# First-layer weights of the routed experts: reordered while they are split, or loaded with a step of eight

## Chip, cores and metric

The kernel runs on one core of one Trainium2 chip. The metric is the device time of one execution in microseconds (us); lower is better. The timed runs and the profiled execution are separate executions of the same program.

## What is computed

An attention with decays gives x (3072 tokens of 384). A first mixture squares a relu between two dense layers (384 to 2048 to 384). Then the part that the change touches: each token is sent to one of 8 experts, 384 tokens to each, by repeatedly taking the largest logit that is left.

```python
def _moe2_ref(x, w_gate, w1, w2):
    N, D = x.shape; E = w_gate.shape[1]; cap = N // E      # 3072, 384, 8 experts, 384 tokens each
    order = np.argsort(-(x @ w_gate).flatten())            # largest logits first
    ...                                                    # each token to the first expert with room
    for e in range(E):
        mask = assigned == e
        h = np.maximum(x[mask] @ w1[e], 0.0)               # w1[e] is 384 x 1024
        out[mask] = h @ w2[e]                              # w2[e] is 1024 x 384
```

## The kernel before

All products keep float32 accuracy by splitting each operand into a high part (float32 rounded to fp32r) and a low part (the remainder). A product is then three matmuls: high times high, high times low and low times high (`passes`, L384). "Splitting" a tile takes two instructions: ScalarE (ACT) writes the high part, and GpSimd (POOL) or VectorE (DVE) subtracts it from the source to give the low part.

**An expert's weights.** `load_w` (L703) fetches one expert's `w1` with an indirect DMA into `w1s`, 128 partitions of 3 x 1024 floats: partition p holds rows 3p, 3p+1 and 3p+2 of `w1[e]`, and each row keeps its 1024 columns in their order. The columns of `w1` become the rows that the second layer sums over. The second layer's `w2s` puts row 8p+j of `w2[e]` in partition p, so layer 1 has to give its outputs in blocks j = 0..7, where block j holds the columns 8q+j, q = 0..127. There is one `w1s` and one `w2s`; the split parts stand in `wbuf`, two buffers of which experts take turns (`w1h`, `w2h`, L905 and L906).

`split_w(k, i)` (L910) splits a piece of expert k's weights: i = 0..2 are the three pieces of `w1` with 128 x 1024 elements, i = 3..6 the four pieces of `w2` with 128 x 768. In the kernel before, the source view of a `w1` piece (L913) goes through the columns with a step of eight floats, so that the part in `wbuf` has the 128 columns of block j side by side. The same view is the source of the high part (L920, ACT) and of the subtraction (L922, POOL or DVE).

**An expert's products.** `layer1(k, j)` (L953) makes block j: nine matmuls (three pieces by three passes) with the weight block as the stationary operand, 128 x 128, and the expert's 384 tokens as the moving one. A relu follows (L965 on ACT, L966 on DVE). `layer2(k, j, i)` (L970) makes nine matmuls per block with the hidden block as the stationary operand.

**Order.** In this stage the order of instructions on PE, DVE, ACT and POOL is written by hand. The loop at L1031 goes over 8 experts and 8 steps each; a step is one `layer1`, then three parts of `layer2` that lag two steps, and between them `side` (L1012) puts in what a table asks for: `s` a piece of the search that assigns tokens of a later expert (L801: DVE compares, PE counts, DVE reads the count, five rounds), `t` a piece of making the list of tokens (L732), `x` the transposes of the gathered tokens (L924), `h`, `p` and `d` the high part of a weight piece and its subtraction on POOL or on DVE, `e` and `w` the result's copy and its indirect DMA from POOL's queue. For expert 1 to 5 the table is EXTRA (L56): of the three `w1` pieces, piece 0 is subtracted on DVE (`d0`), pieces 2 and 1 on POOL (`p2 p1`). For experts 6 and 7 it is EXTRA6 and EXTRA7 (L58, L60), with `d0 d1 p2`. For expert 0 it is START (L63), with `h0 h1 h2`, `d0 d1 p2`.

The same functions serve `general_phase` (L1097), which runs only where the fast assignment fails.

Of the kernel before, what the change touches and what calls it, by code (L numbers as in the profile page):

```python
# [21 lines left out]
CAP = N // E  # L22
# [5 lines left out]
KT = DM // 128  # L28
FT = FF // 128
FT2 = F2 // 128  # L30
# [18 lines left out]
# what each step of an expert does beside its products: s the search of a phase after the next, t the slots  # L49
# of the next, h, p, d weights' parts, x tokens, e, w the former expert's results  # L50
# [37 lines left out]
def moe_kernel(ctx: ExitStack, tc: tile.TileContext, akq, v, w_in, w_out, w_gate, w1, w2, out,  # L88
# [14 lines left out]
    # the last chunk's rows come after one of zeros  # L103
# [14 lines left out]
    # attention inputs of one chunk of 128 tokens: decays, keys and queries with a pair of heads' columns in the  # L118
    # partitions, a column of zeros after each pair's tokens, and values with the tokens in the partitions
# [3 lines left out]
    def load(ch, parts=((0, 3),), eng=sp):  # L123
        """the rows between a pair's heads take the second's first, for whatever is finite will do"""
        for lo, hi in parts:
            for p0, n, r0 in ((0, 64, 0), (64, 48, 48)):
                eng.dma_start(nat[ch % 2][p0:p0 + n, lo:hi, :, :C], akq[ch, r0:r0 + n, lo:hi])
# [4 lines left out]
    # constants that the first chunk needs  # L132
# [30 lines left out]
    # constants that depend on shapes alone  # L163
# [45 lines left out]
    XF, XT = {}, {}  # L209

    def back(x):
        """a row's elements, the last one first"""
        n = x.shape[-1]
        return bass.AP(tensor=x.tensor, offset=x.offset + n - 1, ap=[list(a) for a in x.ap[:-1]] + [[-1, n]])

    def attn(ch, tags="aaaaa"):
        """yields after each of its parts: a decays, q queries and keys, s scores, n keys back, o results"""
# [7 lines left out]
        # products of the decays from each token on, and up to each token over the whole chunk's; what each pair's  # L225
        # start from comes in where the zeros are
# [41 lines left out]
        def result(lo, hi):  # L268
            """what some pairs of heads give, in one bank"""
            py = bank(next(tag), "py")  # L270
            o = py.rearrange("p (a t) -> p a t", a=NP)
            for p in range(lo, hi if c else lo):
                pe.matmul(o[:, p], sa[:, p], qt[:, p], start=p == lo, stop=False)
            for p in range(lo, hi):
                for j in range(2):
                    pe.matmul(o[64 * j:64 * j + D, p], vn[:, 2 * p + j], Pt[:, j, p, :],
                              start=not c and p == lo, stop=p == hi - 1)
            for h in ((slice(0, 128),) if c and hi == NP else (slice(0, D), slice(64, 64 + D))):
                act.activation(x[h, lo:hi, cu * C:(cu + 1) * C], v4(py)[h, lo:hi], AF.Copy)
            if cu == CPU - 1 and hi == NP:  # L280
                # the last pair of heads fills the rows that the other pairs leave
                for o in (0, 64):
                    sp.dma_start(x[o + 48:o + 64, :KT, :], x[o:o + 48, KT, :])
# [63 lines left out]
    def narrow(dst, src):  # L347
        """float64 words (low, high) to float32, of which dst takes the bits"""
        w = src.rearrange("p (n two) -> p n two", two=2)
        lo, hi = w[:, :, 0], w[:, :, 1]  # L350
        dve.tensor_scalar(dst, hi, 3, 0x3FFFFFFF, op0=OP.logical_shift_left, op1=OP.bitwise_and)
        yield
        dve.scalar_tensor_tensor(dst, lo, 29, dst, op0=OP.logical_shift_right, op1=OP.bitwise_or)
        yield
        dve.scalar_tensor_tensor(dst, hi, -(1 << 30), dst, op0=OP.bitwise_and, op1=OP.bitwise_or)
# [75 lines left out]
    def gate(dst, x):  # L431
        """x's rows times the gate's weights"""
        for e in range(E):
            junk = gt_.tile([128, DM], F32, name="gj", bufs=1)
            dve.scalar_tensor_tensor(junk, x, 1.0, wg[:, e], op0=OP.mult, op1=OP.mult, accum_out=dst[:, e:e + 1])  # L435
            yield

    def gate_w():
        """w_out's rows times the gate's weights"""
        for f in range(FT):  # L440
            x = gt_.tile([128, DM], F32, name="gx", bufs=2)
            pool.tensor_tensor(x, wout[:, 0, f, :DM].bitcast(F32), wout[:, 1, f, :DM].bitcast(F32), op=OP.add)
            yield from gate(wr[:, f], x)
        split(lambda i: wlog[:, :, i], wr)
        for i in range(2):
            pool.tensor_copy(wout[:, i, :, DM:], wlog[:, :, i])
        yield

    def share(n):
        """n steps of what the vector engine does for the gate"""  # L450
        while n and tasks:
            if next(tasks[-1], "end") == "end":
                tasks.pop()
            else:
                n -= 1

# [14 lines left out]
    def start_conv(n=1):  # L471
        """the next conversions, in turns so that none waits for itself"""
        cs = [c for _, c in zip(range(n), convs)]
        for _ in range(3):
            for c in cs:
                next(c)
        begun.extend(cs)
# [39 lines left out]
    def logit_range():  # L517
        """the lowest of the logits, but for the last unit's, and what scales them from there to 0..T"""
# [25 lines left out]
    def attend(g):  # L544
        """attention's parts that go with step g"""
        nonlocal done
        n = 0
        while done < (PACE[0] + PACE[1] * g if g < FT else (g + LEAD) * RATE):
            done += 1
            n += 1  # L550
        return n
# [5 lines left out]
    def first_step(g):  # L557
        """a step of the first unit, whose weights come along"""
# [71 lines left out]
    # the rest, in the order of this text  # L630
# [3 lines left out]
    def last_unit():  # L634
        """the last unit's second layer, three products at a time"""
# [50 lines left out]
    # logits of the last unit  # L686
# [33 lines left out]
    def load_half(h):  # L720
        """half of the second layer's weights, for the first expert"""
# [10 lines left out]
    def slots(k, mk, mi, part=False):  # L732
        """token of each of the 384 slots of the expert whose tokens mk marks; mi counts them in a partition;
        in part: the last chunk's are not gathered but marked"""
# [57 lines left out]
    def prep(k):  # L792
        """what a phase's search starts from"""
# [7 lines left out]
    def search(k):  # L801
        """one phase: the greatest threshold with which an expert is full, that expert and its tokens"""
# [20 lines left out]
        for it in range(ITERS):  # L823
# [11 lines left out]
            # G chunks at a time, of which the blocks on the diagonal count  # L835
# [31 lines left out]
        # the threshold as the last comparison had it  # L867
# [36 lines left out]
    half = KT * FT2 * 128 * 2  # L904
    w1h = [w[:, 0:half].rearrange("p (i k j q) -> p i k j q", i=2, k=KT, j=FT2) for w in wbuf]  # L905
# [4 lines left out]
    def split_w(k, i, e="hp"):  # L910
        """a part of an expert's weights: three of the first layer's, four of the second's"""
        if i < KT:
            src = RW[k][0].rearrange("p (k q j) -> p k j q", k=KT, j=FT2)[:, i]  # L913
# [20 lines left out]
    def first_x():  # L934
        """the first expert's tokens: those of the last chunk from where they are, and the others as they come"""
# [17 lines left out]
    def layer1(k, j):  # L953
        wa, xt = w1h[k % 2], XE[k]
        ph = bank("h", "ph3")
        for n, (kt, (wi, xi)) in enumerate(order1):
            pe.matmul(ph[:, :CAP], wa[:, wi, kt, j, :], xt[:, xi, kt, :], start=n == 0, stop=n == 3 * KT - 1)  # L957
# [92 lines left out]
    # whether each phase closed one expert and each expert has its 384 tokens  # L1050
# [29 lines left out]
    def across(x, row, negate=False):  # L1080
        """the greatest of a column's values, in every partition"""
# [7 lines left out]
    def total(x, n):  # L1089
        """the sums of n columns over the partitions, in every partition"""  # L1090
# [6 lines left out]
    def general_phase(L2, gum, gaid, gcap, tok, idr):  # L1097
# [19 lines left out]
        # tokens with the same first choice that come before each token  # L1117
# [16 lines left out]
        # the last token of each expert that fills up, and the first of these tokens  # L1134
# [22 lines left out]
        # the tokens up to that one get their first choice  # L1157
# [59 lines left out]
def arrays(inputs):  # L1217
    """the inputs as the chip reads them"""
    import numpy as _np

    # a chunk's tokens last, a pair's heads before the pairs
# [3 lines left out]
    # rows in the order in which the attention's results come  # L1225
# [30 lines left out]
```

## Time and profile before

| | |
|---|---|
| median of 3 runs | 973.15 us (966.78 to 974.82) |
| span of the profiled execution | 973.9 us |
| PE busy | 833.9 us, 86% of the span |
| DVE busy | 714.5 us, 73% |
| POOL busy | 443.2 us, 46% |
| ACT busy | 327.7 us, 34% |

The span runs from the first to the last instruction of one execution; here it lies 0.75 us above the median of the runs. The first 627 us are attention, the first mixture and the start of the search; the routed experts fill the rest. PE's weight loads (PEld) are instructions of their own that run beside the matmuls. A matmul's time in a row is from its start to its modelled end, and neighbours overlap, so how fast PE goes is read from the distance of starts.

### The profile page before, as it was taken

The page shows a single profiled execution, that of the slowest core. Times are in us where ns is not written, and L with a number is a line of the kernel's source. Part 1 is how long each engine was busy: PE and PEld are TensorE (multiplying, and loading weights), DVE is VectorE, ACT ScalarE, POOL GpSimd, SP SyncE. Part 2 cuts the span into 40 slices and gives each one's busy share as a digit, 9 for nine tenths or more (in the row PEclk, how much of TensorE's full clock was granted, in tenths as well). Part 3 has the DMA queues.
Part 4 walks back from the last instruction along what each step waited for, and adds up shares of the span by engine and source line. Part 5 has one row for each costly group of instructions (what it writes and reads, how often), then busy time and mean ns, then how long its engine had stood idle before and what let it go on. Part 6 is the DMA issues. An engine that isn't in the chain of part 4 may idle for free.

```text
span 973.9 us, 14629 instructions
## 1 busy us (share of the span) xinstructions
PE 833.9 (86%) x5583; PEld 759.1 (78%) x5583; DVE 714.5 (73%) x1594; ACT 327.7 (34%) x581; POOL 443.2 (46%) x389
## 2 busy tenths in 40 slices
PE   6868779888979889899999999748788797988974
PEld 6658678877878779899999998647677685777974
DVE  6878998999998999958542134777687787875540
ACT  1344533223123223233343352224242442425521
POOL 2386763353454444433342442343464556644431
PEclk7888989999999999999999999958798898988988
DMA  9763543112122122232300000314042240422400
GB/s 208 156 190 107 164 110 70 37 28 61 38 43 62 37 43 61 37 72 56 58 25 1 7 25 13 134 37 155 1 178 102 77 171 9 178 84 96 179 25 27
DMA packets 51484, 76.98 MB, mean 79 GB/s; under 512 B 3409, under 2 KB 42706, under 8 KB 49362
## 3 DMA queue, kind: packets, MB, share of 16 engines
q1 hardware_dynamic: 21570, 27.24, 10.3%
q0 software_dynamic: 5520, 34.61, 9.6%
q10 hardware_dynamic: 24320, 14.16, 7.7%
q8 instruction: 45, 0.74, 0.3%
q14 instruction: 29, 0.24, 0.1%
HBM read 65.27 MB, written 9.54 MB: 77 GB/s over the span
## 4 chain that ended last, share of the span: by engine, by line
PE 40%; DVE 36%; issue 4%; ACT 4%; DMA 1%; POOL 1%; POOLq 0%; DVEq 0%; ACTq 0%
DVE gj L435 15%; PE ph L390 9%; PE p L414 7%; PE ph L957 7%; PE py L975 7%; DVE at L861 3%; PE p L641 3%; DVE s L400 3%; DVE wbuf L922 2%; ACT wbuf L920 2%; DVE A L232 1%; DVE thr L827 1%; DVE cm L829 1%; DVE suf L229 1%; DVE Pt L261 1%
## 5 line engine op out<-in xcount | busy, mean ns | idle before, releaser
L390 PE MATMUL ph<-xT,wbuf 128*128 128x384 f32 x1152 | 234.6, 348 | 29.5 <-DVE s L400 12.0
L390 PEld LDWEIGHTS ph<-xT,wbuf 128*128 128x128 f32 x1152 | 207.5, 192 | 40.4 <-DVE s L400 17.4
L402 POOL TENSOR_TENSOR hl<-s,hl 128x384 fp32r<-128x384 f32 x112 | 141.8, 1266 | 184.9 <-ACT hl L401 171.2
L414 PE MATMUL p<-wbuf,hl 128*128 128x384 f32 (+1 forms) x1008 | 205.4, 348 | 4.9 <-POOL hl L402 2.7
L414 PEld LDWEIGHTS p<-wbuf,hl 128*128 128x128 f32 x1008 | 180.0, 193 | 12.2 <-issue 4.2
L975 PE MATMUL py<-wbuf,hl 128*128 128x384 f32 x576 | 133.6, 364 | 0.0
L957 PE MATMUL ph<-xt,wbuf 128*128 128x384 f32 x576 | 122.5, 358 | 10.3 <-DVE xt L932 5.9
L400 DVE SCALAR_TENSOR_TENSOR s<-ph,s 128x384 f32<-128x384 f32 x112 | 62.0, 553 | 89.2 <-ACT s L395 88.8
L401 ACT ACTIVATE hl<-s 128x384 fp32r<-128x384 f32 x112 | 58.8, 525 | 195.7 <-DVE s L400 193.8
L957 PEld LDWEIGHTS ph<-xt,wbuf 128*128 128x128 f32 x576 | 103.7, 198 | 14.1 <-DVE xt L932 6.7
L975 PEld LDWEIGHTS py<-wbuf,hl 128*128 128x128 f32 x576 | 105.6, 201 | 0.7
L435 DVE SCALAR_TENSOR_TENSOR gj<-gx,wg 128x384 f32<-128x384 f32 x128 | 96.1, 751 | 3.1
L395 ACT ACTIVATE s<-ph 128x384 f32<-128x384 f32 x128 | 62.1, 486 | 100.2 <-PE ph L390 70.5
L435 DVE SCALAR_TENSOR_TENSOR gj<-xo,wg 128x384 f32<-128x384 f32 x120 | 78.3, 652 | 12.9 <-ACT xo L422 10.5
L965 ACT ACTIVATE hl<-ph 128x384 fp32r<-128x384 f32 x64 | 31.7, 496 | 135.6 <-PE ph L957 118.6
L922 POOL TENSOR_TENSOR wbuf<-w2s,wbuf 128x768 fp32r<-128x768 f32 x28 | 53.3, 1925 | 44.1 <-ACT wbuf L920 44.1
L966 DVE SCALAR_TENSOR_TENSOR hl<-ph,hl 128x384 fp32r<-128x384 f32 x64 | 35.4, 553 | 38.3 <-ACT hl L965 37.4
L920 ACT ACTIVATE wbuf<-w1s 128x1024 fp32r<-128x1024 f32 x24 | 52.2, 2227 | 2.3 <-DMA w1s<-in_moe_w_dram,wi 2.3
L983 POOL DMA_INDIRECT out_dram<-o,idx x24 | 29.8, 1243 | 50.9 <-ACT o L980 19.0
L838 PEld LDWEIGHTS <-cm 128*128 128x128 bf16 x210 | 8.1, 100 | 49.9 <-DVE cm L829 46.3
L838 PE MATMUL pc<-oh,cm 128*128 128x32 bf16 x210 | 11.3, 182 | 40.1 <-DVE cm L829 40.1
L729 POOL DMA_INDIRECT xg<-x2d,row x24 | 25.1, 1046 | 38.7 <-DVE idx L785 18.2
(204 smaller groups left out, 1229.8 us busy)
## 6 DMA issues: line engine op xcount, KB each, us to landing
rawi<-in_moe_w_in_dram SPq DMA_DIRECT2D x16, 384.0 KB, 3.5
rawo<-in_moe_w_out_dram SPq DMA_DIRECT2D x16, 384.0 KB, 3.7
akq<-in_akq_dram ACTq DMA_DIRECT2D x16, 384.0 KB, 4.5
akq<-in_akq_dram ACTq DMA_DIRECT2D x16, 288.0 KB, 5.8
x2d<-xo SPq DMA_DIRECT2D x24, 192.0 KB, 2.0
v<-in_v_dram ACTq DMA_DIRECT2D x16, 192.0 KB, 2.5
akq<-in_akq_dram SPq DMA_DIRECT2D x7, 384.0 KB, 5.8
akq<-in_akq_dram SPq DMA_DIRECT2D x7, 288.0 KB, 7.3
```

What stands on the lines that cost most here:

```text
L390: pe.matmul(ph[:, :UT], win[:, wi, kt, fs], XT[u][:, xi, kt, :], start=n == 0, stop=n == 3 * KT - 1)
L395: act.activation(s, ph[:, :UT], AF.Relu)
L400: dve.scalar_tensor_tensor(s, ph[:, :UT], 0.0, s, op0=OP.max, op1=OP.mult)
L401: act.activation(hl[:, 0], s, AF.Copy)
L402: (dve if (u, f) == (NU - 1, FT - 1) else pool).tensor_tensor(hl[:, 1], s, hl[:, 0].bitcast(F32), op=OP.subtract)
L414: pe.matmul(PY[u][t][:, :w], hl[:, si, t * C:(t + 1) * C], wout[:, wi, f, :w], start=f == 0 and n == 0, stop=f == FT - 1 and n == 2)
L435: dve.scalar_tensor_tensor(junk, x, 1.0, wg[:, e], op0=OP.mult, op1=OP.mult, accum_out=dst[:, e:e + 1])
L920: act.activation(dst[:, 0], src, AF.Copy)
L922: (dve if "d" in e else pool).tensor_tensor(dst[:, 1], src, dst[:, 0].bitcast(F32), op=OP.subtract)
L957: pe.matmul(ph[:, :CAP], wa[:, wi, kt, j, :], xt[:, xi, kt, :], start=n == 0, stop=n == 3 * KT - 1)
L966: dve.scalar_tensor_tensor(hl[:, 1], ph[:, :CAP], 0.0, hl[:, 0].bitcast(F32), op0=OP.max, op1=OP.subtract)
L975: pe.matmul(PX[k, i][:, :DM], hl[:, hi_, i * 128:(i + 1) * 128], wb[:, wi, j, :], start=j == 0 and n == 0, stop=j == FT2 - 1 and n == 2)
```

## The change

The split keeps the order of the columns: the source view of a `w1` piece is contiguous, and so are both parts in `wbuf`. `layer1` then takes block j out of a piece with a step of eight: 128 columns that stand 8 floats (32 bytes) apart. Nothing else is changed: the number of instructions, their order, sizes and engines stay, and so do the DMAs and the second layer. (Comments were also taken out.)

```diff
-    w1h = [w[:, 0:half].rearrange("p (i k j q) -> p i k j q", i=2, k=KT, j=FT2) for w in wbuf]
+    w1h = [w[:, 0:half].rearrange("p (i k f) -> p i k f", i=2, k=KT) for w in wbuf]
...
         if i < KT:
-            src = RW[k][0].rearrange("p (k q j) -> p k j q", k=KT, j=FT2)[:, i]
+            src = RW[k][0].rearrange("p (k f) -> p k f", k=KT)[:, i]
             dst = w1h[k % 2][:, :, i]
...
         for n, (kt, (wi, xi)) in enumerate(order1):
-            pe.matmul(ph[:, :CAP], wa[:, wi, kt, j, :], xt[:, xi, kt, :], start=n == 0, stop=n == 3 * KT - 1)
+            pe.matmul(ph[:, :CAP], wa[:, wi, kt, j::FT2], xt[:, xi, kt, :], start=n == 0, stop=n == 3 * KT - 1)
```

## Rows read from the trace of the kernel before

**Rows 1.** The page's first part, busy time by engine (share of the span) xinstructions

```profile
PE 833.9 (86%) x5583; PEld 759.1 (78%) x5583; DVE 714.5 (73%) x1594; ACT 327.7 (34%) x581; POOL 443.2 (46%) x389
```

**Rows 2.** Chain of waits from 640 us to the end, shares by line

```profile
by line: PE ph L957 20.5%; PE py L975 19.7%; DVE at L861 8.3%; DVE wbuf L922 6.0%; ACT wbuf L920 5.8%; issue 4.8%; DVE thr L827 4.2%; DVE cm L829 4.0%; PE px L930 2.5%; DVE hl L966 2.5%; DVE aid L874 2.2%; DMA w1s<-in_moe_w_dram,wi 2.1%; PE
```

**Rows 3.** PE's timeline at the end: start us, length us, group

```profile
938.65 1.72 PE L957 MATMUL ph<-xt,wbuf 128*128 128x384 f32 x9
940.21 1.22 PE L975 MATMUL py<-wbuf,hl 128*128 128x384 f32 x6
```

**Rows 4.** Line 920, high parts on ACT: duration ns min/median/max

```profile
L920 ACT ACTIVATE wbuf<-w2s x32: 822/837/1000, 633.0 to 926.6; 128x768 fp32r<-128x768 f32 x32
L920 ACT ACTIVATE wbuf<-w1s x24: 2042/2248/2408, 627.2 to 920.7; 128x1024 fp32r<-128x1024 f32 x24
```

**Rows 5.** ACT's groups by form: busy us, mean ns of one

```profile
L401 ACT ACTIVATE hl<-s 128x384 fp32r<-128x384 f32 x112 | 58.8, 525 | 195.7 <-DVE s L400 193.8 <-PE p L414 1.4
```

**Rows 6.** Line 922, low parts on POOL and DVE: duration ns min/median/max

```profile
L922 POOL TENSOR_TENSOR wbuf<-w2s,wbuf x28: 1792/1834/2573, 636.9 to 928.6; 128x768 fp32r<-128x768 f32 x28
...
L922 POOL TENSOR_TENSOR wbuf<-w1s,wbuf x13: 2857/2982/3282, 634.1 to 923.9; 128x1024 fp32r<-128x1024 f32 x13
L922 DVE TENSOR_TENSOR wbuf<-w1s,wbuf x11: 1995/2232/2352, 629.3 to 920.8; 128x1024 fp32r<-128x1024 f32 x11
...
L922 DVE TENSOR_TENSOR wbuf<-w2s,wbuf x4: 942/2612/5042, 890.9 to 932.1; 128x768 fp32r<-128x768 f32 x4
```

**Rows 7.** PEld's timeline during attention, loads behind short matmuls

```profile
318.08 0.97 PEld L273 LDWEIGHTS py<-qt,sad 112*128 112x128 f32 x8
```

**Rows 8.** ACT's timeline as expert 0's weights come

```profile
627.17 5.96 ACT L920 ACTIVATE wbuf<-w1s 128x1024 fp32r<-128x1024 f32 x3 [0.42 <-DMA w1s<-in_moe_w_dram,wi]
```

**Rows 9.** Windows, line 957 alone: stretch, its us, busy (xcount), granted PE clock

```profile
652.09:662.33 10.24, 7.04 (x21) 5.52 (x19) 0.50 0.01 2
682.81:693.05 10.24, 3.25 (x9) 2.74 (x9) 0.50 0.00 0
773.88:778.38 4.50, 0.44 (x1) 0.44 (x2) 0.50 0.00 0
896.18:901.26 5.08, 2.40 (x7) 2.32 (x8) 0.50 0.00 0
932.23:935.40 3.17, 0.69 (x1) 0.41 (x2) 0.50 0.02 5
```

**Rows 10.** DVE's timeline in the experts' steady stage

```profile
760.27 2.23 DVE L922 TENSOR_TENSOR wbuf<-w1s,wbuf 128x1024 fp32r<-128x1024 f32 x1
...
765.77 6.63 DVE L861 TENSOR_TENSOR at<-n 128x1 f32<-128x1 f32 x1
...
777.97 0.15 DVE L861 TENSOR_TENSOR at<-at,n 128x1 f32<-128x1 f32 x1
```

**Rows 11.** POOL's timeline there

```profile
764.80 5.83 POOL L922 TENSOR_TENSOR wbuf<-w1s,wbuf 128x1024 fp32r<-128x1024 f32 x2
770.60 1.79 POOL L922 TENSOR_TENSOR wbuf<-w2s,wbuf 128x768 fp32r<-128x768 f32 x1
```

**Rows 12.** PE's timeline there; in brackets its idle time and what ended it

```profile
752.11 0.76 PE L772 MATMUL po<-rh,lh 128*128 128x6 bf16 x24
...
773.88 0.35 PE L838 MATMUL pc<-oh,cm 128*128 128x32 bf16 x6 [5.38 <-DVE cm L829]
```

**Rows 13.** DVE's timeline at the start of the experts

```profile
633.80 8.44 DVE L827 TENSOR_SCALAR thr<-iot,n,zero 128x32 f32<-128x32 f32 x1
```

**Rows 14.** Windows of PE's waits: us, busy of PE, PEld, DVE, ACT, POOL, clock

```profile
889.44:896.18 6.74, 1.96 (x9) 1.24 (x9) 6.21 (x6) 3.10 (x7) 4.93 (x3) 0.87 0.00 0
...
924.68:932.23 7.55, 2.07 (x8) 1.25 (x9) 6.97 (x6) 3.13 (x7) 5.74 (x3) 0.76 0.03 12
...
679.84:685.65 5.81, 0.00 (x0) 0.00 (x1) 5.78 (x3) 0.01 (x1) 5.81 (x3) 0.76 0.00 0
```

**Rows 15.** ACT's timeline as expert 6's weights are split (expert 7's is alike)

```profile
881.03 6.68 ACT L920 ACTIVATE wbuf<-w1s 128x1024 fp32r<-128x1024 f32 x3
```

## Prediction

> **What bounds the kernel now.** I read the engine shares first: PE leads with 86%, DVE has 73% [rows 1]. A share of 86% leaves open whether the change's stage waits for PE, so the second view is the chain of waits over that stage. There PE's two layers hold 20.5% and 19.7%, and DVE and ACT work that is not products holds much of the rest, the split itself 6.0% (L922) and 5.8% (L920) [rows 2]. So the stage has two limits in turn: PE's stream of products, and waits in which the split stands in the way of the search. The change touches both, in opposite directions. Third, the pace of the stream: from the start of nine `layer1` matmuls to the next group 1.56 us pass, 173 ns for each pair of load and matmul [rows 3].
>
> **Part 1: the pieces of w1 read in order.** On ACT a contiguous piece of 384 takes 525 ns [rows 5] and one of 768 takes 837 ns [rows 4]: 0.81 ns per element and 0.21 us fixed. A contiguous piece of 1024 would then take 1.05 us; with the step of eight it takes 2.25 us. Saved: 1.20 us a piece, 24 pieces, 29 us of ACT. On DVE 768 contiguous elements take 0.94 us at best, so 1024 at most 1.26; saved 1.0 of 2.23 us, 11 pieces. On POOL 768 take 1.83 us, so 1024 some 2.45; saved 0.5 of 2.98 us, 13 pieces [rows 6]. These are engine times; what the end gets of them is decided by the waits:
>
> - *Start, expert 0.* Three ACT pieces follow each other for 5.96 us [rows 8], two DVE pieces follow them at about 2.0 us each (the shortest in rows 6), and then a comparison's threshold, which is 0.3 us of work elsewhere, takes 8.44 us [rows 13]: it begins at 633.8, POOL's first subtraction at 634.1. While POOL subtracts, DVE stands. The first ACT piece ends about 1.0 us earlier, the two DVE pieces save 0.75 each: DVE would be there 2.5 us before POOL begins, and POOL is done 0.5 us sooner. Bounds 0.5 and 3.5, taken 3.0, since an earlier DVE gets a round of the search in.
> - *Expert 1.* PE waits 5.81 us while POOL is busy all through [rows 14]. An ACT piece ahead of a relu (1.1), the DVE piece (1.0) and two POOL pieces (half of 1.1) shorten that by 2.7.
> - *Experts 2 to 5.* DVE's addition of one element, 0.15 us in its next round, takes 6.63 us and ends at 772.40 [rows 10], where POOL's three subtractions end (772.39) [rows 11]; PE waits 5.38 us for the comparison behind it [rows 12]. Two of the three are `w1` pieces: 1.1 us less. The DVE piece before it (760.27) also saves 1.0 us, but DVE then only stands earlier at the same subtractions, so I cost that at nothing; if POOL came late it would be worth 1.0.
> - *Experts 6 and 7.* PE waits 4.78 (6.74 less 1.96) and 5.48 us (7.55 less 2.07) [rows 14]. Behind them are three ACT pieces in 6.68 us [rows 15], then DVE and POOL. Three times 1.2 and 0.5: 4.1 each.
>
> Sum without any cost on PE: 3.0 + 2.7 + 4 x 1.1 + 2 x 4.1 = 18.3 us.
>
> **The clock.** After each of these waits PE runs a stretch at a granted 0.50, the lower of its two levels: 4.50 us in experts 2 to 5 (773.88), 5.08 and 3.17 us in 6 and 7 [rows 9]. At half clock a stretch that PE fills loses half its length. Where the wait all but disappears (6 and 7), I give back 2.5 + 1.6 = 4.1 us. In 2 to 5 each stretch is worth 2.25 us, 9.0 in all; whether they go depends on how short the waits get.
>
> **Part 2: 576 weight loads with a step of eight floats.** No weight load of the trace has a step, so its price is bounded. Today a load hides: eight loads of 128 columns behind short matmuls take 0.97 us, less the last one's 0.19 us that is 111 ns each [rows 7], below the 173 ns of a pair. A load may grow by 62 ns for nothing; that is the lower end, a cost of zero. For the upper end I take the nearest rows, the other engine that reads this very pattern. ACT needs (5.96/3 - 0.21)/1024 = 1.73 ns per element when little else runs [rows 8], 1.99 in the median and 2.14 at the slowest [rows 4], against 0.81 in order. For 128 columns that is 222, 255 and 274 ns, that is 49, 82 and 101 ns over the pair's 173. DVE's 2.0 to 2.23 us for the same 1024 elements come to 1.8 to 2.1 ns, fixed time taken off alike: two engines with different work arrive at one price, which speaks for the memory as its cause, not for the engine. So I take the middle of the first two, 65 ns a pair. An outer end: a load that does not overlap at all with the one before, 255 less 111 = 144 ns.
>
> [...]
>
> Some 42 of the 576 pairs run at half clock (21, 9, 7 and 1 in the stretches of rows 9, and about one for each of experts 2 to 5) [rows 9], where a pair takes about twice as long (21 in 7.04 us) and hides the load. 534 x 65 ns = 34.7 us of PE time, 0.585 us a step.
>
> **The sum.** Not all of it shows, since slower steps run while PE would have waited:
>
> - Start: 42 full-clock pairs, +2.7, less 3.0: -0.3.
> - Expert 1: 72 pairs, +4.7, less 2.7: +2.0.
> - Experts 2 to 5: 71 pairs, +4.6; less 1.1; and between POOL's trigger (the token list's matmuls at 752.11 [rows 12]) and DVE's stand PE makes three steps, which now give POOL 1.75 us more of a lead. +1.75 each, +7.0.
> - Expert 6: 65 pairs, +4.2, less the whole wait of 4.78 (4.1 from the pieces, the rest under slower steps): -0.6. Expert 7: +4.6 less 5.48: -0.9.
> - Clock: 4.1 given back in 6 and 7, and half of the 9.0 in 2 to 5, whose waits fall from 5.38 to about 2.5: -8.6.
>
> -0.3 + 2.0 + 7.0 - 0.6 - 0.9 - 8.6 = -1.4. From the profiled 973.9 us that is 972.5, and the profiled span is the runs' median (973.15) within 0.1%: 972 us.
>
> **The cases.**
>
> *Forecast: the load is paid at the memory's price, gain and cost cancel.* At 49 ns the 534 pairs cost 8.5 less (964), at 82 ns 9 more (981); with all or none of the steady clock stretches given back 4.5 either way. Own range 959 to 987. For it: two engines with the same price. Against: PE's port may be another. Chance 0.45.
>
> *Rival 1, faster: the step costs PE nothing,* because the load stays under 173 ns (under 1.35 ns a column). Then 18.3 + 4.1 = 22.4 us are gained: 952; without clock and start's bonus 958, with the steady stretches too 943. For it: PE takes its 384 moving columns in 173 ns, 0.45 ns each, against ACT's 0.81 in order, so its reading is quicker than ACT's. Chance 0.33. [...]
>
> *Rival 2, slower: PE's load is dearer than on ACT,* since two streams, weights and tokens, read at once. From 101 ns a pair (+19 us on the forecast, 991; 1000 if no clock stretch goes) to 144 ns (+42, 1014). It passes the 1% mark once a pair grows by some 85 ns. For it: ACT's price already rises from 1.73 to 1.99 ns when the other engines run. Against: loads and matmuls overlap well now. Chance 0.22; 0.02 of it is the case that the change doesn't do what it says, the pieces staying at 2.2 us because something else than the step makes them long, which the contiguous `w2` pieces speak against.
>
> **Chances and range.** One per cent of 973 is about what a measurement of this kernel can tell from no change (the three runs spread 0.8%): 963.4 to 982.9. Faster: 0.30 from rival 1 and 0.08 from the forecast's cheap end, 0.38. Slower: 0.21 from rival 2 and 0.08 from the dear end, 0.29. Within: 0.33. The range 948 to 1000 leaves out rival 1's lower end (about 0.10) and rival 2 beyond the lost clock (0.10).
>
> **What would show it.** ACT's `w1` pieces at 1.05 us, DVE's near 1.26, POOL's near 2.45: part 1. The distance of starts within nine `layer1` matmuls late in the kernel, free of waits: 173 ns is rival 1, 220 to 255 the forecast, more rival 2; `layer2` as now in each. PE's waits for L829 in experts 2 to 5 near 2.5 us, near 4.3 under rival 1. The number of half-clock stretches tells the clock's term. The prediction is wrong in its mechanism if the pieces don't shorten, or if the one-element addition no longer stands for POOL at all.

## The result, and the profile after

The changed kernel takes 983.2 us in the median (979.11 to 985.55, 7 runs), the kernel before 973.15 us (966.78 to 977.53, 7 runs). The ratio is 1.012 with a 95% interval of 1.0078 to 1.0163: slower by 1.2%. The forecast was 972 us, no change; the time lies inside the range of 948 to 1000. The profiled execution has a span of 977.2 us.

Engine shares: PE has more to do, ACT, DVE and POOL less (compare [rows 1]).

```profile
PE 857.0 (88%) x5583; PEld 788.3 (81%) x5583; DVE 698.0 (71%) x1594; ACT 300.0 (31%) x581; POOL 435.4 (45%) x389
```

The chain of waits from 640 us to the end, by line: `layer1` (L957) has doubled its share from 20.5% to 41.3%, and the split (L920, L922), 11.8% before, is no longer among the shares shown (compare [rows 2]).

```profile
by line: PE ph L957 41.3%; PE py L975 29.0%; DVE cm L829 10.2%; PE px L930 2.9%; PE pb L851 1.7%; PE pc L838 1.6%; PE po L772 1.2%; DVE hl L966 1.0%; PE pb L856 1.0%; DVE thr L827 1.0%; ACT hl L965 0.9%; issue 0.7%; DVE mk L885 0.5%; DVE xt
```

Part 1, the pieces: the split's lines, duration in ns as min/median/max. ACT's `w1` piece went from 2248 to 1050 ns (forecast 1050), DVE's from 2232 to 1216 (1260), POOL's from 2982 to 2383 (2450); compare [rows 4, 6].

```profile
L920 ACT ACTIVATE wbuf<-w1s x24: 1040/1050/1059, 622.2 to 923.4; 128x1024 fp32r<-128x1024 f32 x24
...
L922 POOL TENSOR_TENSOR wbuf<-w1s,wbuf x13: 2337/2383/3152, 626.6 to 924.7; 128x1024 fp32r<-128x1024 f32 x13
L922 DVE TENSOR_TENSOR wbuf<-w1s,wbuf x11: 1202/1216/1227, 623.3 to 923.7; 128x1024 fp32r<-128x1024 f32 x11
```

Part 2, the loads: PE's timeline late in the kernel (start us, length us, group). From the start of nine `layer1` matmuls to the next group 2.18 us pass, 242 ns a pair where [rows 3] had 173: 69 ns more, forecast 65.

```profile
950.39 2.33 PE L957 MATMUL ph<-xt,wbuf 128*128 128x384 f32 x9
952.57 0.69 PE L975 MATMUL py<-wbuf,hl 128*128 128x384 f32 x3
```

So both sizes were right and the sum was not. Where the time went shows in the lengths of the stages, from one expert's first `layer1` matmul to the next one's, in us, worked out from the starts in the two traces. The forecast's terms are put in the stage in which they fall.

| stage | before | after | difference | forecast |
|---|---|---|---|---|
| first piece split to expert 0 | 23.44 | 20.46 | -3.0 | -3.0 |
| expert 0 (wait for expert 1's pieces) | 44.98 | 40.22 | -4.8 | 0.0 |
| expert 1 | 41.23 | 44.84 | +3.6 | |
| expert 2 | 41.12 | 45.48 | +4.4 | |
| expert 3 | 41.03 | 46.52 | +5.5 | |
| expert 4 | 40.94 | 44.77 | +3.8 | |
| experts 1 to 4 together | 164.32 | 181.61 | +17.3 | +2.6 |
| expert 5 | 30.08 | 34.15 | +4.1 | +4.6 |
| expert 6 | 35.29 | 32.40 | -2.9 | -3.1 |
| expert 7 to the end | 48.62 | 46.21 | -2.4 | -2.5 |
| sum | 346.73 | 355.05 | +8.3 | -1.4 |

Ahead of these stages the profiled execution after is 5.0 us shorter (622.16 against 627.17 us); the change touches nothing there. The lengths of start, 5, 6 and 7 came as forecast (of the start, 6 and 7 the runs below show other reasons). Experts 1 to 4 did not: 14.7 us more than the forecast. PE's wait for the comparison (L829) was to fall from 5.38 us [rows 12] to about 2.5. It is 5.45. POOL's, DVE's and PE's timelines around it in expert 2:

```profile
756.32 4.68 POOL L922 TENSOR_TENSOR wbuf<-w1s,wbuf 128x1024 fp32r<-128x1024 f32 x2
760.95 1.80 POOL L922 TENSOR_TENSOR wbuf<-w2s,wbuf 128x768 fp32r<-128x768 f32 x1
```

```profile
755.46 0.30 DVE L827 TENSOR_SCALAR thr<-iot,n 128x32 f32<-128x32 f32 x1
755.79 7.78 DVE L829 TENSOR_TENSOR cm<-m,thr 128x768 bf16<-128x768 f32 x1
```

```profile
755.14 2.51 PE L957 MATMUL ph<-xt,wbuf 128*128 128x384 f32 x9
757.49 0.69 PE L975 MATMUL py<-wbuf,hl 128*128 128x384 f32 x3
763.63 0.34 PE L838 MATMUL pc<-oh,cm 128*128 128x32 bf16 x6 [5.45 <-DVE cm L829]
```

POOL's three subtractions are shorter (6.43 us against 7.59 in [rows 11]), but DVE now stands at a comparison, 7.78 us for 0.96 us of work. It is that of the third of the five search rounds; in [rows 10] DVE had the third round's count already and stood on the way to the fourth comparison. And PE, which had 3.70 us of work in hand when POOL began (764.80 to 768.50), now has 1.86 (756.32 to 758.18). Before: 7.59 of block, 1.49 until the count starts, less 3.70: 5.38. After: 6.43 + 0.88 - 1.86 = 5.45. What the shorter pieces gave, the work in hand took back. In PE's order (matmuls counted in the traces from expert 2's first `layer1`), POOL's block began, in the kernel before, when PE had started 192, and PE stopped after 213, ahead of the fourth count. Now it begins at 174, so POOL does have a longer lead, but the count that is stuck is the third, and PE stops after 181. To the fourth count it would have had 39 matmuls in hand; to the third it has 7.

The half-clock stretches behind the four waits (line 957 alone; stretch, its length, PE and PEld busy, granted clock) are 34.1 us long in all; before, they were four of 6.83 us, of which the 4.50 us with PE at work stand in [rows 9].

```profile
715.52:722.35 6.83, 0.00 (x0) 0.00 (x0) 0.50 0.01 2
759.89:770.13 10.24, 2.97 (x9) 2.77 (x9) 0.50 0.01 2
807.68:817.92 10.24, 3.27 (x9) 2.77 (x9) 0.50 0.00 0
852.05:858.88 6.83, 0.00 (x0) 0.00 (x0) 0.50 0.00 0
```

### The profile page after: what moved, and what is told of

Read it like the earlier page. It is cut to its first block, busy times and chain, and to the rows that moved or that the text cites. A ratio compares the mean times of both kernels' runs of the same rounds, so it can differ in the third digit from the quotient of the medians.

```text
span 977.2 us, 14629 instructions
## 1 busy us (share of the span) xinstructions
PE 857.0 (88%) x5583; PEld 788.3 (81%) x5583; DVE 698.0 (71%) x1594; ACT 300.0 (31%) x581; POOL 435.4 (45%) x389
## 4 chain that ended last, share of the span: by engine, by line
PE 50%; DVE 31%; issue 2%; ACT 2%; DMA 1%; POOL 1%; POOLq 0%; DVEq 0%; ACTq 0%
DVE gj L435 16%; PE ph L957 14%; PE py L975 10%; PE ph L390 9%; PE p L414 7%; DVE cm L829 4%; DVE s L400 3%; PE p L641 2%; DVE A L232 1%; DVE suf L229 1%; DVE Pt L261 1%; DVE thr L827 1%; PE px L930 1%; DVE kt L236 1%; PE py L276 1%
## 5 line engine op out<-in xcount | busy, mean ns | idle before, releaser
L957 PE MATMUL ph<-xt,wbuf 128*128 128x384 f32 x576 | 158.8, 423 | 0.0
L957 PEld LDWEIGHTS ph<-xt,wbuf 128*128 128x128 f32 x576 | 145.9, 336 | 1.6 <-issue 1.2
L975 PE MATMUL py<-wbuf,hl 128*128 128x384 f32 x576 | 130.4, 357 | 0.0
L975 PEld LDWEIGHTS py<-wbuf,hl 128*128 128x128 f32 x576 | 103.5, 197 | 0.7
L922 POOL TENSOR_TENSOR wbuf<-w2s,wbuf 128x768 fp32r<-128x768 f32 x28 | 53.4, 1927 | 66.0 <-ACT wbuf L920 66.0
L829 DVE TENSOR_TENSOR cm<-m,thr 128x768 bf16<-128x768 f32 x28 | 56.2, 2007 | 1.0
L983 POOL DMA_INDIRECT out_dram<-o,idx x24 | 27.8, 1159 | 47.1 <-ACT o L980 19.8
L729 POOL DMA_INDIRECT xg<-x2d,row x24 | 23.1, 962 | 46.0 <-DVE idx L785 29.2
L838 PE MATMUL pc<-oh,cm 128*128 128x32 bf16 x210 | 11.3, 182 | 33.5 <-DVE cm L829 33.5
```

The source lines that it names most:

```text
L829: dve.tensor_tensor(cm, m2[:, :, None].to_broadcast([128, NCH, T]), thr[:, None, :].to_broadcast([128, NCH, T]), op=OP.is_ge)
L922: (dve if "d" in e else pool).tensor_tensor(dst[:, 1], src, dst[:, 0].bitcast(F32), op=OP.subtract)
L957: pe.matmul(ph[:, :CAP], wa[:, wi, kt, j::FT2], xt[:, xi, kt, :], start=n == 0, stop=n == 3 * KT - 1)
L975: pe.matmul(PX[k, i][:, :DM], hl[:, hi_, i * 128:(i + 1) * 128], wb[:, wi, j, :], start=j == 0 and n == 0, stop=j == FT2 - 1 and n == 2)
```

## Experiments

**Theory:** the change is two independent parts, pieces that save and stepped loads that cost 65 to 69 ns a pair, and experts 1 to 4 keep their wait because, with slower steps, POOL's block falls one search round earlier, where PE has less work in hand until it needs the count that is stuck. **Rivals:** the loss comes from the shorter pieces themselves (a new order of search and subtractions), or slower steps hide under the waits after all, as the forecast had it.

### The two halves alone

The halves are undone by the layout in which the inputs stand in memory before the kernel starts (`arrays`, which lays out other weights in the same way); the routed part computes the same.

`r1_order_free`: short pieces, contiguous loads.

```diff
-            pe.matmul(ph[:, :CAP], wa[:, wi, kt, j::FT2], ...)
+            pe.matmul(ph[:, :CAP], wa[:, wi, kt, j * 128:(j + 1) * 128], ...)
...
+    a["moe2_w1"] = inputs["moe2_w1"].reshape(E, DM, 128, FT2).transpose(0, 1, 3, 2).reshape(E, DM, F2)
```

> The columns of w1 are put into the order of the blocks before the kernel starts (the inputs' layout), so pieces are read in order and loads are contiguous too. Theory (the stepped load alone is what costs): the pair of load and matmul is back at 173 ns, the pieces stay at 1.05 us on ACT, 1.2 on DVE, 2.4 on POOL, and the time is 951 to 956 us, 17 to 22 below the kernel before. Rival (the short pieces themselves moved the order of search and subtractions so that it waits more): no better than 965 us, with PE's waits for the comparison in experts 2 to 5 still at 5.4 us.

Measured: 956.15 us against 971.39 for the kernel before beside it, ratio 0.9864 (0.9807 to 0.9921). The pair is at 173 ns, ACT's piece at 1.05 us. PE's wait in expert 2 is 1.04 us shorter than before, as the prediction had costed two shorter POOL pieces (1.1):

```profile
760.05 0.34 PE L838 MATMUL pc<-oh,cm 128*128 128x32 bf16 x6 [4.34 <-DVE cm L829]
```

The short pieces alone are a gain of 15 us. That is 0.15 us above the theory's 951 to 956, and the rival (waits still at 5.4) is out. POOL's block stays where it was, ahead of the fourth count: it begins after 193 of expert 2's matmuls, and PE stops after 213. In experts 6 and 7 the short pieces alone leave most of PE's wait, 7.5 us of 10.3 ([rows 14]):

```profile
PE ph L957 <- DVE xt L932: 7.5, 2, 4.4
```

`r2_step_load_alone`: long pieces, stepped loads, on the kernel before.

```diff
-            pe.matmul(ph[:, :CAP], wa[:, wi, kt, j, :], ...)
+            pe.matmul(ph[:, :CAP], wa[:, wi, kt].rearrange("p j q -> p (j q)")[:, j::FT2], ...)
...
+    a["moe2_w1"] = inputs["moe2_w1"].reshape(E, DM, FT2, 128).transpose(0, 1, 3, 2).reshape(E, DM, F2)
```

> The pieces are read with the step as before (2.2 us on ACT), and the loads have a step of eight as well; the inputs' layout undoes the one for the other. It is the other half of the change alone. Theory of two independent parts: pair 240 ns, and the time is that of before plus what the changed kernel lies above r1_order_free, 1000 to 1005 us. Rival (a slower PE stream hides under the waits that the long pieces leave): PE's waits in experts 2 to 7 get shorter by 2 us or more each, and the time stays under 992 us.

Measured: 1000.85 us against 971.39, ratio 1.0319 (1.0265 to 1.0372), pair at 242 ns. The loads alone cost 29 us, within the theory's 1000 to 1005. With r1's gain of 15 that makes +14, against the +10 measured for both: additive to within 4 us. The rival asked for shorter waits in experts 2 to 7. In experts 1 to 4 they got longer, 7.35 us in place of 5.38; only the waits at the start of experts 6 and 7, 4.78 and 5.48 before [rows 14], shrank, to 2.6 us in all, none of them above 0.8. PE's wait in expert 2:

```profile
776.91 0.34 PE L838 MATMUL pc<-oh,cm 128*128 128x32 bf16 x6 [7.35 <-DVE cm L829]
```

As in the changed kernel, the block comes one round earlier. POOL begins after 176 of expert 2's matmuls and PE stops after 181, ahead of the third count. DVE stands at the threshold (L827) of that round's comparison:

```profile
767.63 8.22 DVE L827 TENSOR_SCALAR thr<-iot,n 128x32 f32<-128x32 f32 x1
```

So the stepped loads alone move the block by a round; the short pieces alone (r1) do not. Slower steps hide a wait in one place (experts 6 and 7, 10.3 us down to 2.6) and lengthen it in another (5.38 us up to 7.35). That is the step at which the forecast went wrong, seen with the pieces held fixed.

### What a step costs a load

As the changed kernel, with the columns of a block 2 or 4 floats apart and the inputs laid out to match (`r3_step_two` and `r4_step_four`; the second has 4 and 512 where the line below has 2 and 256).

```diff
-            pe.matmul(ph[:, :CAP], wa[:, wi, kt, j::FT2], ...)
+            pe.matmul(ph[:, :CAP], wa[:, wi, kt, j // 2 * 256:(j // 2 + 1) * 256][:, j % 2::2], ...)
```

> As the changed kernel, but with the inputs laid out so that a block's columns stand two floats (8 bytes) apart. [...] Rival (any step costs a load its rate): pair at 240 ns, time as the changed kernel. Rival (it goes with the distance): in between, near 180 to 190 ns.

> A block's columns stand four floats (16 bytes) apart. [...]

Measured, in one run each: step 2, 955.58 us and a pair of 174 ns, as in order; step 4, 980.14 us and 233 ns. Step 8, the changed kernel, has 242 ns. PE's timelines of r3 and of r4, late in the kernel: (931.29 - 929.72)/9 = 174 ns, (955.81 - 953.71)/9 = 233 ns.

```profile
929.72 1.73 PE L957 MATMUL ph<-xt,wbuf 128*128 128x384 f32 x9
931.29 1.04 PE L975 MATMUL py<-wbuf,hl 128*128 128x384 f32 x5
```

```profile
953.71 2.26 PE L957 MATMUL ph<-xt,wbuf 128*128 128x384 f32 x9
955.81 0.52 PE L975 MATMUL py<-wbuf,hl 128*128 128x384 f32 x2
```

Nearly all of the price, 59 of 68 ns, comes between 8 and 16 bytes; the next doubling adds 9 ns. Neither "any step costs" nor "it goes with the distance" fits. Why the price sets in between these two steps, no run shows.

### The wait in experts 1 to 4

`r7_later_block`: one high part is made later on ACT, so that POOL begins later.

```diff
-EXTRA = ((4, 2, "h0"), (4, 4, "h1"), (5, 3, "d0 h2"), (6, 0, "h3"), (6, 3, "x0"), ...
+EXTRA = ((4, 2, "h0"), (4, 4, "h1"), (5, 3, "d0"), (6, 0, "h3"), (6, 2, "h2"), (6, 3, "x0"), ...
```

> The changed kernel, with the high part of the third w1 piece for experts 1 to 5 made one step later on ACT, so that POOL's three subtractions begin some 2.5 us later against PE's stream. Theory (the wait is POOL's end less the time PE has work in hand, and the changed kernel lost a step of that work because POOL's block now falls one search round earlier): the wait moves back from step 6 to step 7 and falls to 3 to 4.5 us, 972 to 979 us. Rival (the wait is the length of POOL's block whenever it comes): 5.4 us again, 981 to 986 us.

Measured: 974.14 us, ratio to the kernel before 1.0029 (1.0004 to 1.0054), where the changed kernel had 1.012. The block is as long as in the changed kernel (6.46 us), and the wait falls to 3.20 us. It is back at the fourth count: POOL begins after 195 of expert 2's matmuls, PE stops after 213. POOL's and PE's timelines in expert 2:

```profile
762.53 4.70 POOL L922 TENSOR_TENSOR wbuf<-w1s,wbuf 128x1024 fp32r<-128x1024 f32 x2 [2.93 <-ACT wbuf L920]
767.20 1.79 POOL L922 TENSOR_TENSOR wbuf<-w2s,wbuf 128x768 fp32r<-128x768 f32 x1
```

```profile
765.97 0.69 PE L975 MATMUL py<-wbuf,hl 128*128 128x384 f32 x3
769.86 0.34 PE L838 MATMUL pc<-oh,cm 128*128 128x32 bf16 x6 [3.20 <-DVE cm L829]
```

PE had 4.13 us of work in hand (762.53 to 766.66) in place of 1.86: 2.27 us more, and the wait is 2.25 us shorter. With blocks of one length (6.43 and 6.46 us), the wait fell by what the work in hand at POOL's start gained. (DVE's instructions are held one after the other here, for 1.52, 2.23 and 2.50 us; the last one ends 0.82 us after the block in both.)

`r5_dve_subtracts`: POOL's two `w1` subtractions go to DVE, for experts 1 to 5.

```diff
-EXTRA = (..., (6, 4, "p2 p1"), (7, 3, "x2 p3"),
+EXTRA = (..., (6, 4, "d2 d1"), (7, 3, "x2 p3"),
```

> The changed kernel, with the two w1 subtractions that POOL makes for experts 1 to 5 given to DVE at the same places of the table. Theory (PE's 5.45 us wait in experts 1 to 4 is DVE standing for POOL's three subtractions in a row, of which one of 1.8 us is left): waits of 2 us or less, half-clock stretches there gone or shorter, 963 to 971 us. Rival (DVE's 2.4 us of added work delay the search as much as the standing did): waits of 4 us or more, 978 to 986 us.

Measured: 956.03 us, ratio 0.9837 (0.9794 to 0.9879): below even the 963 to 971 of the theory. The waits for L829 between 650 and 950 us sum to 5.9 us, none over 0.9 (total, times, longest), and there is no half-clock stretch between 652 us and the end of the last products (mean granted clock of the profiled execution 0.964, 0.945 in the changed kernel):

```profile
PE pc L838 <- DVE cm L829: 5.9, 9, 0.9
```

`r9_before_dve`: the same edit on the kernel before.

> The kernel before, with the two w1 subtractions of experts 1 to 5 on DVE; against r5_dve_subtracts it shows the change without POOL's block in experts 1 to 5. Theory (then PE's stream sets the pace there, and the stepped loads cost their full 65 to 69 ns a pair): 942 to 952 us, r5_dve_subtracts 4 to 14 us slower than this. Rival (the long pieces on DVE, three times 2.2 us, make the search the limit): waits of 3 us or more in experts 1 to 4, 956 us or above, and the change costs nothing there.

Measured: 955.40 us, ratio 0.9813 (0.9777 to 0.9849), over the theory's 942 to 952 and 0.6 us under the rival's 956. In the same window the waits are 19.8 us in all; the longest in each of experts 1 to 4 is 2.9 to 3.6 us. With three pieces of 2.2 us on DVE the search is late even with POOL's two `w1` pieces gone; with pieces of 1.2 us and the same loads the waits are 2.0 us (r8, below).

```profile
PE pc L838 <- DVE cm L829: 19.8, 10, 3.6
```

So the rival holds in the main: with this assignment the change is worth nothing either way (956.0 against 955.4, ratios to the kernel before 0.9837 and 0.9813, intervals overlapping). The stepped loads' cost and the short pieces' gain then meet, as the forecast had it for the kernel as it stood.

### The clock behind the waits

`r6_pe_kept_busy`: matmuls of ones, their results unused, fill PE's wait in the changed kernel.

```diff
                     layer2(k, j, i)
+                if i == 0 and s == 6 and 1 <= e <= 4:
+                    busy = bank("h", "busy")
+                    for _ in range(20):
+                        pe.matmul(busy[:, 0:128], ones, ones, start=True, stop=True)
                 side(e, s, 3 + i)
```

> The changed kernel, with 20 matmuls of ones (some 4.3 us, their results unused) put into PE's order where it waits in experts 1 to 4. They move no other work and prolong PE's own, if anything. Theory (the half-clock stretches behind the waits cost real time): the stretches in experts 1 to 4 vanish, PE's groups behind the waits run at full pace, 970 to 975 us. Rival (what follows a wait is paced by the search and not by PE's clock, so it costs nothing): less than 4 us gained, or a loss, at 980 us or above.

Measured: 975.61 us, ratio 1.0031 (1.0002 to 1.006), 0.6 us above the theory's 970 to 975. The half-clock stretches in experts 1 to 4 are gone (mean granted clock of the profiled execution 0.957 against 0.945). Expert 2's window, first in the changed kernel, then here (length, busy of PE, PEld, DVE, ACT, POOL, granted clock):

```profile
727.68:773.16 45.48, 39.75 (x238) 35.14 (x237) 32.76 (x87) 12.67 (x22) 21.48 (x14) 0.89 0.27 96
```

```profile
731.40:774.88 43.48, 42.20 (x278) 38.07 (x277) 32.65 (x86) 12.64 (x22) 21.50 (x14) 1.00 0.28 101
```

Over experts 1 to 4 the stages sum to 172.8 us against 181.6. So some 9 us of the changed kernel are half-clock time behind these waits, at the same waits (5.46 us in expert 2, with the ones in it, where 5.45 stood empty): the search ends no sooner, but PE runs its queue behind it at a granted 1.00, where expert 2 of the changed kernel has 0.50 for 10.24 us.

### A kernel that beats both

`r8_order_free_dve`: the layout of r1 with the assignment of r5.

> r1_order_free (contiguous pieces and loads by the inputs' layout) with the two w1 subtractions of experts 1 to 5 on DVE as well. Theory (both are independent gains): PE's waits in experts 1 to 4 fall from 4.3 to 1.5 us or less, 940 to 949 us. Rival (DVE becomes what the search waits for): 953 us or above.

Measured: 936.58 us, ratio 0.9655 (0.9607 to 0.9704), below the expected 940 to 949. PE's waits in experts 1 to 4 are 2.0 us each, where 1.5 or less was expected. It needs the inputs in another layout, which the changed kernel does not; with the inputs as they are, r5 and r9 are the best that was run, 956.0 and 955.4 us. Against r5, which differs from r8 by the loads alone, the stepped loads cost 19 us.

## Why the prediction was right or wrong

- **The pieces: right.** 1050, 1216 and 2383 ns against 1050, 1260 and 2450 forecast.
- **The load: right.** ACT's price for the same pattern, taken as the memory's, gave 65 ns a pair; it was 69. That the memory sets it, not the engine, was the author's estimate from two engines with one price, and no run shows it; the runs with steps of 2 and 4 floats show only by how much the pair grows, to 174 and 233 ns.
- **Expert 5: right within 0.6 us.**
- **Experts 6 and 7: the lengths were right, the shares were not.** The waits and their half-clock stretches vanished, as forecast. But 4.1 us of each wait were put down to the pieces. Of 10.3 us in both together, the short pieces alone leave 7.5 (r1), the stepped loads alone 2.6 (r2). That the sum came out is in part luck.
- **Start: the 3.0 us came, but not in the way that was forecast.** DVE was to be ahead of POOL and get a round of the search in. It was 0.34 us ahead (626.24 against 626.58) and stood through POOL's subtractions as before, 7.99 us where [rows 13] have 8.44; POOL's first subtraction followed ACT's first piece after 4.4 us instead of 6.9. And two kernels with long pieces, r2 and r9, have starts of 19.7 us, shorter than the 20.46 with short ones. That the pieces gave these 3.0 us is not shown; the number was luck.
- **Experts 2 to 5's weights (split in the stages of experts 1 to 4): wrong, and this decided the result.** The step that failed is "PE makes three steps, which now give POOL 1.75 us more of a lead", 4 x 1.75 = 7.0 us counted as cover. The lead came: POOL's block begins 18 matmuls earlier in PE's order. On POOL's queue only the list's gathers and issues of results stand between the list and the block; from the list's matmuls to POOL's start 12.7 us passed before (752.11 to 764.80) and 11.3 after (745.01 to 756.32), though PE's steps had become longer. But the forecast kept the instruction at which DVE stands. The rounds of the search go along with PE's order, so a block that comes earlier in that order catches an earlier round, and PE needs the third count 32 matmuls before the fourth. Work in hand fell from 3.70 to 1.86 us where it should have grown by 1.75. r2 shows it with long pieces (wait 5.38 to 7.35 us), r1 that short pieces do not do it, r7 by bringing the wait back to the fourth count (5.45 to 3.20).
- **The clock in the same stages: wrong as a consequence.** The forecast gave back 4.5 us because the waits were to fall to about 2.5 us; they stayed at 5.45, and the stretches grew from 27.3 to 34.1 us. r6 puts the price of these stretches in the changed kernel at about 9 us.
- **Expert 0: a gain missed.** 0.0 forecast, -4.8 measured. Its `layer1` pairs at half clock fell from 28 to 13 (counted in the traces), and the wait ahead of expert 1's weights from 5.81 us to 2.38. I had costed the wait and left out the clock behind it, though I used the same term elsewhere. The 2.7 us for slower loads did not show in the length either: with loads in order the stage takes 40.34 us (r1), with the step 40.22.
- **Balance:** four waits of 5.45 us in place of some 2.5, +11.6 (7.0 us of cover that did not come, the rest for the work in hand that was lost, net); +4.5 for the clock; -1.4 in the same stages, not settled; -4.8 in expert 0; -0.2 in the others: 9.7 us between -1.4 and +8.3. The profiled spans differ by only 3.3 us, for the 5.0 us ahead of the stages; the stages' 8.3 lies in the 7.6 to 15.9 us that the runs' ratio gives.
- **A reading.** With ACT's 0.21 us taken off, DVE's 2.0 to 2.23 us [rows 6] are 1.7 to 2.0 ns per element, not 1.8 to 2.1. The 65 ns do not rest on it.
- **The rivals.** Rival 1's case is r1 in all but the load: 952 were worked out, 956 measured. With 128 columns each, a pair took 173 ns in order (r1) and 242 with the step (changed kernel). Rival 2 named the right side, but by a dearer load; the load was not dearer.

## What to carry to other kernels

When work on one queue becomes slower, list for each known wait whether the event that ends it moves along with that queue. If it doesn't, the event falls on an earlier place in the slower queue's order. Look there for what it will catch, and how much work that queue has in hand until it needs the thing caught. The slower work covered the wait only where the same thing was caught as before (r7, 3.20 us against 5.38); in the changed kernel and in r2 it was a search round earlier, and the wait stayed or grew (5.45 and 7.35). For a layout there are two readers to count: here the step cost 29 us at PE's loads (r2), and 15 us were gained where the split was rid of it (r1), so a strided read belongs with the engine that has slack, or in a layout outside the kernel; a step of two floats cost a weight load nothing (r3, 174 ns a pair against 173).

## What the hardware showed that was not expected

- A pair of a 128-column float32 weight load and its matmul took 173 to 174 ns with a step of 1 or 2 floats (r1, r3), 233 ns with 4 (r4) and 242 ns with 8 (changed kernel).
- DVE's two-input comparison of 0.96 us, started 0.53 us before POOL's first subtraction, ended only 0.82 us after POOL's third (7.78 us in all, expert 2 of the changed kernel). Being first did not protect it, and it was not done in the 6.43 us of POOL's three instructions.
- It was not always so. In expert 2 of r7 POOL makes its three subtractions in a row as well, from 762.53 to 768.99 us, and DVE gets through three instructions meanwhile, each held for 1.4 to 1.9 us beyond its work, two of them below. What decides between the two cases is open.

```profile
765.05 2.23 DVE L827 TENSOR_SCALAR thr<-iot,n,at 128x32 f32<-128x32 f32 x1
767.31 2.50 DVE L829 TENSOR_TENSOR cm<-m,thr 128x768 bf16<-128x768 f32 x1
```
